# Three edits to a convolution and routed-experts kernel: smaller matmul tiles for the last 15 blocks, fp32r transposes of the expert pages, and five scatters a round

## The chip, the cores and the metric

The kernel runs on one core of a Trainium2 chip. A time is the device time of one launch in microseconds (us). The core has a matrix engine (TensorE, PE in the profile, with its weight loads listed apart as PEld), a vector engine (VectorE, DVE), an activation engine (ScalarE, ACT), a general one (GpSimd, POOL) and SyncE (SP), which here only issues transfers. Sixteen DMA engines move data between HBM and the on-chip memory SBUF. Matmuls write to PSUM, from which ACT and DVE copy.

## The reference

Two layers, one after the other, all in float32.

1. A long convolution for a batch of 4 sequences of 10048 positions and 128 channels: a filter is made by a small network from position embeddings (`relu(pos_emb @ w1) @ w2`, times a decaying window), `u = x * v` is convolved with it along the sequence by a Fourier transform of length 2 * 10048, and the result is multiplied by `x`.
2. Routed experts over the resulting 40192 tokens of 128 channels: a token chooses one of 4 groups by the largest of 4 logits, then one of that group's 4 experts, and its output is `g_w * e_w * (relu(x @ w1[g, e]) @ w2[g, e])`, with 1024 hidden units; the weights are the two softmax values of the choice.

## The kernel before

**The transform.** A sequence is cut into 79 blocks of 128 positions (10112, padded). The Fourier transform of length 157 * 128 is done in two factors: first over the 79 blocks (matrices `fa`, `fm`, `fr`), then over the 128 positions in a block (`c_b`). A channel's 79 blocks are split as 64 + 15, so that a channel's 64 main blocks fill half of the 128 rows of TensorE; the 15 that are left over are packed for three channels into one set of rows.

**Stages.** The filter's spectrum is made first. Then for each batch element b = 0..3 the kernel runs a *channel stage* and a *frequency stage*, and at the end one more channel stage for the last inverse:

- Channel stage (the loop over `OUTS`, lines 262 to 283). `OUTS` has 22 units of channels: 20 of six and two of four. They are worked in 11 pairs. For a pair the kernel transposes the back-transformed data of batch b-1 (`turned`, L704 and L707), runs the first factor of batch b for the pair's two units (`dft_unit`, L416 and L423), and the inverse first factor of batch b-1 (`inverse_rest`, L719; `inverse_blocks`, L740). The product `x * v` and its folding run a few units ahead on DVE (`run_ahead`, L487, L496, L497).
- Frequency stage (`middle` and `back`, 40 steps of two of the 79 frequencies): second factor (L506), multiplication by the filter's spectrum on DVE (L672, L675), sums on POOL (L673, L676), inverse second factor (L685), copy back on ACT (L692). The routing of the tokens of the batch element before runs inside it (`chosen`, `ranked`).

`dft_unit` writes a unit of six channels to two PSUM banks, three channels each. Its main part issues 12 matmuls (L416), each of 64 rows by 64 columns, 158 columns of the moving matrix `fm`. Its rest (L423) issues four matmuls of 64 by 64, in which one set of rows holds the 15 left-over blocks of three channels and the moving matrix `fr` has 3 * 158 = 474 columns, zero but for the blocks of the channel in question. In the profile a matmul of float32 operands shows as two records, each of all its columns. Then four copies take the result from PSUM: two main parts on ACT, two rests on DVE (L438).

**Scatters.** When the tokens of a batch element are ranked, their rows (130 numbers: the token, its place, its weight) are scattered by POOL into `prow`, a memory of pages sorted by expert. There are 79 scatters to a batch element, 128 rows each (L383), and `scatter(n)` sends up to n that are due. They are written into the program between the other work: in the channel stage one ahead of each unit and `1 + (j >= 6)` after each unit (line 274), so four to a pair in the first three pairs and six in each later one; in the frequency stage one in three of every four steps. POOL takes its work in the order of the program: a scatter that is late holds up the sums L673 and L676 behind it. A scatter also waits for the last copy written ahead of it (`pace`). By counting the turns in the code, 54 of a batch element's 79 scatters are written into the channel stage (0, 2, 4 and then 6 in each of 8 pairs) and 25 into the first 33 steps of the frequency stage. They are the rows of the batch element two before, so this concerns b = 2 and 3; the scatters of the last two elements fall into the last channel stage and the experts.

**Experts.** A page is 512, 384 or 256 rows of one expert. `load` brings it to SBUF (`xg`), `turn` transposes it 128 rows at a time (L1306, one matmul with the page as weights and the identity as the moving matrix), `rows` splits the transposed tokens into a high part in fp32r and a low part, and `first` and `second` (L1351 to L1353, L1371 to L1373) form every product as three fp32r matmuls of the parts. `turn_back` transposes the result (L1385). Every PE instruction of this phase keeps the order written down.

**Matrices.** `fm` and `fr` are loaded by POOL's queue at the top of the program (L556, L557), among the loads that the filter's network waits for.

Of the kernel before, what the change touches and what calls it, by code (L numbers as in the profile page):

```python
# [77 lines left out]
def make_consts():  # L78
# [14 lines left out]

    fr = np.zeros((2, KM, 2, GD, 2 * NB))
    for i in range(GD):
        fr[:, 16 * i : 16 * i + NB - KM, :, i] = fa[KM:].reshape(-1, 2, 2 * NB)
# [61 lines left out]
class Kernel:  # L158
# [62 lines left out]
    def conv(self, ctx, right):  # L221
# [7 lines left out]
        self.fm = cp.tile([128, 2, 2 * NB], F32, name="fm")  # L229
        self.fr = cp.tile([128, 2, GD, 2 * NB], F32, name="fr")  # L230

# [18 lines left out]
        for b in range(self.nbat + 1):  # L250
# [11 lines left out]
            for j, (d0, n) in enumerate(OUTS):  # L262
                if b > 0 and j % 2 == 0:
                    tts = self.turned(d0, min(2 * GI, D - d0))
                for i in range(j, j + 2) if not last and j % 2 == 0 else ():
                    self.run_ahead(b, i, made, folded)
                    self.scatter(1)
                    self.dft_unit(*folded[i])
                if b > 0:
                    if j % 2 == 0:  # L270
                        pos = self.inverse_rest(min(2 * GI, D - d0), tts)
                    self.inverse_blocks(b - 1, xy, d0, n, tts, pos[j % 2], j % 2)
                if not last:
                    self.scatter(1 + (j >= 6))
                if last:
                    next(weights, None)
                    if j == 8:
                        self.scatter(sum(1 for s in self.scatters if s[0] < self.nbat - 2))
                        self.all[0].load(self.rows)
                for _ in range(3 if last else 1):  # L280
                    next(routing, None)
                if last:
                    self.scatter(1 + j % 2)
# [123 lines left out]

    def dft_unit(self, b, eo, d0, n):

# [3 lines left out]
        for i in range(m):  # L413
            for h, hs in enumerate(HALVES):
                for ps, rs in zip(pss, HALVES):
                    ins = nc.tensor.matmul(  # L416
                        ps[hs, i], eo[rs, i, hs], self.fm[rs, h], start=i == 0, stop=False
                    )
                    if b and d0 == i == h == 0 and ps is pss[0]:
                        self.tc.keep_in_program_order(ins)  # L420
        for h, hs in enumerate(HALVES):
            for ps, rs in zip(pss, HALVES):
                nc.tensor.matmul(  # L423
                    ps[hs, :m].rearrange("p d k -> p (d k)"),
                    eo[rs, m, hs],
                    self.fr[rs, h, :m].rearrange("p d k -> p (d k)"),
                    start=False,
                    stop=True,
                )
        for r, ps in enumerate(pss):  # L430
            ds_ = slice(d0 + r * m, d0 + r * m + m)
# [102 lines left out]
    def network(self, ctx, eo):  # L534
# [11 lines left out]
        for j, m in groups(64, 4):  # L546
# [7 lines left out]
            if j == 16:  # L554
                nc.sync.dma_start(self.fa.rearrange("p h k -> p (h k)"), d["c_fa"])
                nc.gpsimd.dma_start(self.fm.rearrange("p h k -> p (h k)"), d["c_fm"])  # L556
                nc.gpsimd.dma_start(self.fr.rearrange("p h c k -> p (h c k)"), d["c_fr"])  # L557
        w1 = self.parts(tp, w1, "w1", lo=nc.vector)
# [522 lines left out]
    def moe(self, ctx, right, routing):  # L1081
# [4 lines left out]
        ]  # L1086
        self.sp = pools[0]
        self.weights = self.moe_weights(
            right.enter_context(tc.tile_pool(name="second", bufs=1, side="right", reuse_waits="tile")), 1
# [160 lines left out]
class Page:  # L1250
# [37 lines left out]
    def load(self, pool=None):  # L1288
        k, nc, pg = self.k, self.k.nc, self.k.pages
        self.xg = (pool or k.sp).tile([128, self.th, RW], F32, tag="xg", name="xg", bufs=1 if pool else XG)  # L1290
        at = (pool or k.sp).tile([1, 1], I32, tag="at", name="at", bufs=1 if pool else 4)
        k.tc.keep_in_program_order(nc.vector.tensor_copy(at, pg.entry(*self.at)[:, 1:2]))
        row = nc.sync.value_load(at, min_val=0, max_val=pg.none)
        src = k.d["prow"][self.skip :][ds(row, self.rows_)]
        ins = nc.sync.dma_start(self.xg, src.rearrange("(p h) c -> p h c", h=self.th))
        k.tc.keep_in_program_order(ins)
# [4 lines left out]
    def turn(self):  # L1301

        k, nc = self.k, self.k.nc
        self.px = k.psx.tile([128, self.rows_], F32, tag="px", name="px")
        for h in range(self.th):
            k.fix(nc.tensor.transpose(self.px[:, h * 128 : h * 128 + 128], self.xg[:, h, 0:128], k.ident))  # L1306

    def rows(self):
# [8 lines left out]
        self.weight = k.sp.tile([128, self.th], F32, tag="wt", name="wt", bufs=4)  # L1317
        k.fix(nc.vector.tensor_copy(self.to, self.xg[:, :, 128]))
        k.fix(nc.vector.tensor_copy(self.weight, self.xg[:, :, 129]))

# [116 lines left out]
def layout(x, v, pos_emb, w1, w2, moe_w_group, moe_w_expert, moe_w1, moe_w2):  # L1437
# [44 lines left out]

    def unit(a, n):

        u = np.zeros((2, KM, n + 1, 2, 128), np.float32)
        for r in range(2):
            u[r, :, :n] = a[:KM, r * n : r * n + n]
            u[r, : 16 * n, n] = a[KM:, r * n : r * n + n].transpose(1, 0, 2, 3).reshape(16 * n, 2, 128)
        return u

    m = {
        "xv_in": np.concatenate([unit(xv[:, d0 : d0 + n], n // 2).ravel() for xv in xvs for d0, n in OUTS]),
        "x_out": c(
# [38 lines left out]
```

## Time and profile before

| | us |
|---|---|
| median of 3 runs | 1886.09 (1885.25 to 1890.03) |
| the profiled execution: its own time | 1890.19 |
| its span in the profile | 1888.4 |
| PE busy | 1796.0 (95%) |
| DVE busy | 1362.8 (72%) |
| ACT busy | 1237.2 (66%) |
| POOL busy | 977.0 (52%) |

A busy PE is not a PE at its peak: a matmul's record lasts from its start until its last result, and the next begins before that. So the cost of a matmul is read from the distance between starts, not from its mean duration. The granted clock of TensorE in the rows is a share of 2.4 GHz.

### The profile page before, as it was taken

Reading aid. Unit: us, or ns where it says so; the run is one execution under the profiler, and the core shown is the slowest. Engines: PE = TensorE matmul, PEld = TensorE weight load, DVE = VectorE, ACT = ScalarE, POOL = GpSimd, SP = SyncE. Lnnn points to the kernel's source line nnn. Section 1 sums busy time; section 2 is a strip of 40 time slices with the busy share of each in tenths; the row PEclk is TensorE's granted clock in tenths of the full one; section 3 lists DMA queues with packets and bytes.
Section 4 is the critical chain, followed back from the end, with each engine's and each line's share of the span. In section 5 each row is a group of like instructions: output and inputs, shape, how many; then the busy total and the mean of one; then the engine's idle time right before and its main releaser. Section 6 shows DMA issues by size and latency. Waiting matters only on the chain.

```text
span 1888.4 us, 43889 instructions
## 1 busy us (share of the span) xinstructions
PE 1796.0 (95%) x14662; PEld 1489.7 (79%) x14662; DVE 1362.8 (72%) x3068; ACT 1237.2 (66%) x2708; POOL 977.0 (52%) x1105
## 2 busy tenths in 40 slices
PE   7988999999989898988899999999999999999998
PEld 6866888777867686776688888888888888889998
DVE  5385777688758874873779877777777777777886
ACT  5474367436734574456677777777777777777886
POOL 3101820574899478967255556677666333333354
PEclk9999999999989998999899999999999999999999
DMA  4477975986889688865563333444443223222342
GB/s 135 141 281 261 306 242 167 315 265 222 264 294 307 212 275 284 304 210 188 179 210 113 112 111 122 156 135 135 123 132 117 90 89 91 89 87 84 97 130 90
DMA packets 201596, 338.18 MB, mean 179 GB/s; under 512 B 26904, under 2 KB 88445, under 8 KB 201360
## 3 DMA queue, kind: packets, MB, share of 16 engines
q1 hardware_dynamic: 170448, 274.87, 45.5%
q0 software_dynamic: 21408, 44.88, 6.7%
q10 hardware_dynamic: 9504, 15.54, 2.9%
q8 instruction: 118, 1.93, 0.4%
q14 instruction: 118, 0.97, 0.2%
HBM read 260.22 MB, written 75.53 MB: 178 GB/s over the span
## 4 chain that ended last, share of the span: by engine, by line
PE 53%; DVE 2%; ACT 1%; issue 1%; DMA 0%; SPq 0%; POOL 0%; ACTq 0%; DVEq 0%; POOLq 0%
PE py L1373 8%; PE py L1371 8%; PE ph L1351 8%; PE ph L1353 8%; PE py L1372 8%; PE ph L1352 8%; PE ptm L1385 2%; PE px L1306 2%; PE po L740 1%; PE po L719 1%; PE ptr L821 1%; DMA wf<-m_w 0%; PE pt L707 0%; PE plt L829 0%; ACT tt L709 0%
## 5 line engine op out<-in xcount | busy, mean ns | idle before, releaser
L1360 DVE SCALAR_TENSOR_TENSOR hl<-ph,hh 128x512 fp32r<-128x512 f32 (+1 forms) x656 | 441.6, 674 | 157.3 <-ACT hh L1359 152.2
L1397 POOL DMA_INDIRECT out<-os,to x320 | 318.4, 995 | 415.9 <-ACT os L1392 343.0
L1359 ACT ACTIVATE hh<-ph 128x512 fp32r<-128x512 f32 (+1 forms) x656 | 388.1, 592 | 170.4 <-PE ph L1353 140.1
L383 POOL DMA_INDIRECT prow<-stg,adr x316 | 331.5, 1049 | 133.3 <-issue 68.1
L1351 PE MATMUL ph<-xh,wh 128*128 128x512 f32 (+2 forms) x720 | 280.4, 389 | 6.0 <-ACT wh L1333 6.0
L1353 PE MATMUL ph<-xh,wl 128*128 128x512 f32 (+2 forms) x720 | 265.5, 369 | 1.6 <-DVE ep L1268 1.3
L1371 PE MATMUL py<-hh,wh 128*128 128x512 f32 (+2 forms) x720 | 264.5, 367 | 0.0
L1373 PE MATMUL py<-hh,wl 128*128 128x512 f32 (+2 forms) x720 | 264.4, 367 | 0.0
L1352 PE MATMUL ph<-xl,wh 128*128 128x512 f32 (+2 forms) x720 | 264.3, 367 | 0.0
L1372 PE MATMUL py<-hl,wh 128*128 128x512 f32 (+2 forms) x720 | 263.2, 366 | 0.0
L673 POOL TENSOR_TENSOR y<-t 128x256 f32<-128x256 f32 (+1 forms) x160 | 120.5, 753 | 210.1 <-DVE t L672 205.7
L692 ACT COPY z<-pbp 128x512 f32<-128x512 f32 x128 | 74.9, 585 | 190.0 <-PE pbp L685 190.0
L506 PE MATMUL psb<-z,bt 128*128 128x256 f32 x640 | 168.2, 391 | 28.9 <-issue 15.4
L685 PE MATMUL pbp<-y,bp 128*128 128x256 f32 x632 | 164.2, 383 | 3.4 <-POOL y L676 3.1
L672 DVE TENSOR_TENSOR t<-psb,ht 128x512 f32<-128x512 f32 (+1 forms) x160 | 108.8, 680 | 75.4 <-POOL y L676 21.8
L506 PEld LDWEIGHTS psb<-z,bt 128*128 128x128 f32 x640 | 119.3, 198 | 52.3 <-issue 27.5
L1353 PEld LDWEIGHTS ph<-xh,wl 128*128 128x128 f32 x720 | 136.3, 189 | 24.0 <-DVE ep L1268 1.8
L1351 PEld LDWEIGHTS ph<-xh,wh 128*128 128x128 f32 x720 | 136.6, 190 | 22.3 <-ACT wh L1333 6.7
L1372 PEld LDWEIGHTS py<-hl,wh 128*128 128x128 f32 x720 | 135.9, 189 | 21.8
L1373 PEld LDWEIGHTS py<-hh,wl 128*128 128x128 f32 x720 | 135.8, 189 | 21.8
L1371 PEld LDWEIGHTS py<-hh,wh 128*128 128x128 f32 x720 | 135.9, 189 | 21.3
L1352 PEld LDWEIGHTS ph<-xl,wh 128*128 128x128 f32 x720 | 137.1, 190 | 15.9
(230 smaller groups left out, 3480.9 us busy)
## 6 DMA issues: line engine op xcount, KB each, us to landing
ws<-m_w SPq DMA_DIRECT2D x180, 256.0 KB
xv<-xv_in SPq DMA_DIRECT2D x80, 512.0 KB
ht<-hspec SPq DMA_DIRECT2D x156, 256.0 KB
bt<-c_b SPq DMA_DIRECT2D x95, 256.0 KB
bp<-c_bp SPq DMA_DIRECT2D x76, 256.0 KB
xyd<-xy SPq DMA_DIRECT2D x76, 256.0 KB
stg<-xyd SPq DMA_DIRECT2D x76, 256.0 KB
xg<-prow SPq DMA_DIRECT2D x66, 260.0 KB
```

Source lines behind the costliest of these rows:

```text
L383: ins = self.nc.gpsimd.indirect_dma_start(self.d["prow"], bass.IndirectOffsetOnAxis(ap=u.adr[:, t : t + 1], axis=0), u.rows[:, t - u.t0], ...
L506: nc.tensor.matmul(ps[:, i].rearrange("p s d -> p d s"), bt[:, i], self.frequency(k0 + i, 1)[:, :, 0], start=True, stop=True,)
L685: nc.tensor.matmul(by_part[:, i], bp[:, i], y[:, i], start=True, stop=True,)
L1351: k.fix(nc.tensor.matmul(ph[:, j], wh, self.xh, start=True, stop=False))
L1352: k.fix(nc.tensor.matmul(ph[:, j], wh, self.xl, start=False, stop=False))
L1353: k.fix(nc.tensor.matmul(ph[:, j], wl, self.xh, start=False, stop=True))
L1359: k.fix(nc.scalar.activation(hh, ph, AF.Relu))
L1360: k.fix(nc.vector.scalar_tensor_tensor(hl, ph, 0.0, hh.bitcast(F32), ALU.max, ALU.subtract))
L1371: k.fix(nc.tensor.matmul(self.py, wh, hh, start=(c == 0), stop=False))
L1372: k.fix(nc.tensor.matmul(self.py, wh, hl, start=False, stop=False))
L1373: k.fix(nc.tensor.matmul(self.py, wl, hh, start=False, stop=(c == NC - 1)))
L1397: ins = k.nc.gpsimd.indirect_dma_start(k.d["out"], bass.IndirectOffsetOnAxis(ap=self.to[:, h : h + 1], axis=0), o, None, bounds_check=k.nt ...
```

## The change

- The rest of the first factor is issued once for a pair of units. `dft_unit` is split into `dft_main`, `dft_rest` and `dft_leave`. The four PSUM banks of the two units each get a row group of 32: eight matmuls of 32 rows by 64 columns with 2 * 158 columns for the first two channels of each bank, then, where units have three channels to a bank, eight of 16 rows by 64 columns with 158 columns for the third. `fr` and the layout of the input follow (`both` in place of `unit`). The copies of both units come after the rest.
- The transposes of a page's tokens (`turn`) take fp32r operands: `xg` is an fp32r tile, an fp32r copy of the identity is made once, and `px` is fp32r in PSUM. Those who read them afterwards read the same bits as float32.
- `fm` and `fr` are loaded by SP's queue, behind the loads of the filter's network.
- In the channel stage `scatter(1 + j % 2)` takes the place of `scatter(1 + (j >= 6))`: five to every pair.

```diff
-                for i in range(j, j + 2) if not last and j % 2 == 0 else ():
-                    self.run_ahead(b, i, made, folded)
-                    self.scatter(1)
-                    self.dft_unit(*folded[i])
+                if not last and j % 2 == 0:
+                    units = []
+                    for i in range(j, j + 2):
+                        self.run_ahead(b, i, made, folded)
+                        self.scatter(1)
+                        units.append(self.dft_main(*folded[i]))
+                    self.dft_rest(b, units)
...
-                    self.scatter(1 + (j >= 6))
+                    self.scatter(1 + j % 2)
...
+    def dft_rest(self, b, units):
+
+        nc = self.nc
+        (one, _, m, low), (two, _, _, high) = units
+        banks = [(ps, slice(32 * g, 32 * g + 32)) for g, ps in enumerate(low + high)]
+        k = min(m, 2)
         for h, hs in enumerate(HALVES):
-            for ps, rs in zip(pss, HALVES):
+            for ps, rs in banks:
                 nc.tensor.matmul(
-                    ps[hs, :m].rearrange("p d k -> p (d k)"),
-                    eo[rs, m, hs],
-                    self.fr[rs, h, :m].rearrange("p d k -> p (d k)"),
+                    ps[hs, :k].rearrange("p d k -> p (d k)"),
+                    one[rs, m, hs],
+                    self.fr[rs, h, :k].rearrange("p d k -> p (d k)"),
                     start=False,
-                    stop=True,
+                    stop=m == k,
                 )
+        for h, hs in enumerate(HALVES) if m > k else ():
+            for ps, rs in banks:
+                rs = slice(rs.start, rs.start + 16)
+                nc.tensor.matmul(ps[hs, k], two[rs, m, hs], self.fr[rs, h, 0], start=False, stop=True)
+        for _, d0, m, pss in units:
+            self.dft_leave(b, d0, m, pss)
...
             if j == 16:
                 nc.sync.dma_start(self.fa.rearrange("p h k -> p (h k)"), d["c_fa"])
-                nc.gpsimd.dma_start(self.fm.rearrange("p h k -> p (h k)"), d["c_fm"])
-                nc.gpsimd.dma_start(self.fr.rearrange("p h c k -> p (h c k)"), d["c_fr"])
+            if j == 60:
+                nc.sync.dma_start(self.fm.rearrange("p h k -> p (h k)"), d["c_fm"])
+                nc.sync.dma_start(self.fr.rearrange("p h c k -> p (h c k)"), d["c_fr"])
...
+        self.identr = self.sp.tile([128, 128], F32R, tag="identr", name="identr", bufs=1)
+        nc.scalar.copy(self.identr, self.ident)
...
-        self.px = k.psx.tile([128, self.rows_], F32, tag="px", name="px")
+        px = k.psx.tile([128, self.rows_], F32R, tag="px", name="px")
         for h in range(self.th):
-            k.fix(nc.tensor.transpose(self.px[:, h * 128 : h * 128 + 128], self.xg[:, h, 0:128], k.ident))
+            k.fix(nc.tensor.transpose(px[:, h * 128 : h * 128 + 128], self.xg[:, h, 0:128], k.identr))
+        self.px = px.bitcast(F32)
```

## Rows read from the trace of the kernel before

**Rows 1.** Busy by stretch: length, PE, PEld, DVE, ACT, POOL (records), clock, DMA, GB/s.

```profile
133.20:178.80 45.60, 41.01 (x684) 30.85 (x680) 28.15 (x68) 26.43 (x95) 0.00 (x0) 0.96 0.81 285
...
250.10:332.90 82.80, 82.79 (x1617) 67.31 (x1617) 58.60 (x144) 61.93 (x129) 0.49 (x1) 1.00 0.63 188
332.90:429.90 97.00, 92.42 (x579) 71.47 (x577) 76.40 (x160) 40.87 (x94) 63.00 (x83) 1.00 0.89 292
...
516.90:626.20 109.30, 95.76 (x581) 72.75 (x577) 79.62 (x160) 41.43 (x95) 99.45 (x126) 0.95 0.91 297
...
937.00:1750.00 813.00, 812.82 (x3897) 676.63 (x3896) 613.20 (x1295) 614.16 (x1248) 418.07 (x439) 1.00 0.38 119
```

**Rows 2.** Timeline, one pair of b = 2: start, length, engine, line, operation, records.

```profile
471.11 1.86 PE L740 MATMUL po<-fi,tt 128*64 128x79 f32 x48
...
477.94 0.98 PE L719 MATMUL po<-fi,tt 64*64 64x158 f32 x24
...
478.86 1.86 PE L740 MATMUL po<-fi,tt 128*64 128x79 f32 x48
...
480.65 0.55 PE L704 MATMUL pt<-ident,zr 128*128 128x128 f32 x3
...
482.30 0.97 ACT L709 COPY tt<-pt 128x384 f32<-128x384 f32 x2
...
482.44 1.04 PE L416 MATMUL psa<-fm,eo 64*64 64x158 f32 x24
...
483.29 0.98 PE L423 MATMUL psa<-fr,eo 64*64 64x474 f32 x8
...
484.09 0.99 PE L416 MATMUL psa<-fm,eo 64*64 64x158 f32 x24
...
484.89 0.98 PE L423 MATMUL psa<-fr,eo 64*64 64x474 f32 x8
```

**Rows 3.** Timeline of POOL in the channel stage of b = 2.

```profile
451.02 1.42 POOL L383 DMA_INDIRECT prow<-stg,adr  x1 [21.39 <-ACT oo L750]
...
469.45 0.98 POOL L383 DMA_INDIRECT prow<-stg,adr  x1 [0.30 <-ACT z L438]
...
516.38 0.98 POOL L383 DMA_INDIRECT prow<-stg,adr  x1 [0.30 <-DVE zr L438]
```

**Rows 4.** Timeline, start of the frequency stage of b = 2; in brackets the idle time before.

```profile
530.45 0.74 POOL L673 TENSOR_TENSOR y<-t 128x256 f32<-128x256 f32 x1
...
532.01 2.04 PE L506 MATMUL psb<-z,bt 128*128 128x256 f32 x4 [7.71 <-issue]
```

**Rows 5.** Timeline of PE, frequency stages of b = 1 and of b = 2.

```profile
350.50 1.02 PE L685 MATMUL pbp<-y,bp 128*128 128x256 f32 x4
...
543.74 1.02 PE L685 MATMUL pbp<-y,bp 128*128 128x256 f32 x4
```

**Rows 6.** Chain that ended last: four transposes of one page.

```profile
1044.59 0.44 PE px L1306 x4
```

**Rows 7.** Weight loads by line: total busy, mean ns of one, idle before.

```profile
L1351 PEld LDWEIGHTS ph<-xh,wh 128*128 128x128 f32 x720 | 136.6, 190 | 22.3 <-ACT wh L1333 6.7
...
L1306 PEld LDWEIGHTS px<-ident,xg 128*128 128x128 f32 x320 | 40.0, 140 | 8.9
...
L1062 PEld LDWEIGHTS pe<-ident,lst 128*1 128x1 f32 x20 | 0.7, 82 | 3.2 <-DVE yt L754 2.8 <-issue 0.4
```

**Rows 8.** Timeline of PE in a page of 256 rows.

```profile
1820.13 0.28 PE L1351 MATMUL ph<-xh,wh 128*128 128x256 f32 x1
1820.25 0.28 PE L1352 MATMUL ph<-xl,wh 128*128 128x256 f32 x1
```

**Rows 9.** Timeline of ACT at the start of the program.

```profile
9.05 0.46 ACT L524 CAST p<-pt 128x320 fp32r<-128x320 f32 x1 [3.24 <-DMA pt<-pos_t]
```

**Rows 10.** DMA issues: the size of `fr`.

```profile
fr<-c_fr POOLq DMA_DIRECT2D x1, 474.0 KB
```

**Rows 11.** Busy time by stretch at the start of the program.

```profile
6.00:8.00 2.00, 0.90 (x2) 0.50 (x2) 0.43 (x2) 0.00 (x0) 0.00 (x0) 1.00 0.98 327
```

More of the change, by code (lines that the diff above doesn't have):

```diff
@@ L91, in make_consts @@
     ).reshape(NB, -1)
-    fr = np.zeros((2, KM, 2, GD, 2 * NB))
-    for i in range(GD):
+    fr = np.zeros((4, 32, 2, 2, 2 * NB))
+    for i in range(2):
         fr[:, 16 * i : 16 * i + NB - KM, :, i] = fa[KM:].reshape(-1, 2, 2 * NB)
@@ L229, in conv @@
         self.fm = cp.tile([128, 2, 2 * NB], F32, name="fm")
-        self.fr = cp.tile([128, 2, GD, 2 * NB], F32, name="fr")
+        self.fr = cp.tile([128, 2, 2, 2 * NB], F32, name="fr")
         self.z = zp.tile([128, D, KM, 2], F32, name="z")
@@ L406, in clear, with dft_main @@
         return ins
-    def dft_unit(self, b, eo, d0, n):
+    def dft_main(self, b, eo, d0, n):
         nc, m = self.nc, n // 2
@@ L420, in dft_unit, with dft_leave @@
                         self.tc.keep_in_program_order(ins)
+        return eo, d0, m, pss
+    def dft_rest(self, b, units):
[3 more added lines that the diff above has]
+        k = min(m, 2)
         for h, hs in enumerate(HALVES):
-            for ps, rs in zip(pss, HALVES):
+            for ps, rs in banks:
                 nc.tensor.matmul(
-                    ps[hs, :m].rearrange("p d k -> p (d k)"),
-                    eo[rs, m, hs],
-                    self.fr[rs, h, :m].rearrange("p d k -> p (d k)"),
+                    ps[hs, :k].rearrange("p d k -> p (d k)"),
+                    one[rs, m, hs],
+                    self.fr[rs, h, :k].rearrange("p d k -> p (d k)"),
                     start=False,
-                    stop=True,
+                    stop=m == k,
                 )
+        for h, hs in enumerate(HALVES) if m > k else ():
[4 more added lines that the diff above has]
+            self.dft_leave(b, d0, m, pss)
+    def dft_leave(self, b, d0, m, pss):
+        nc = self.nc
         for r, ps in enumerate(pss):
@@ L1289, in load @@
         k, nc, pg = self.k, self.k.nc, self.k.pages
-        self.xg = (pool or k.sp).tile([128, self.th, RW], F32, tag="xg", name="xg", bufs=1 if pool else XG)
+        self.xg = (pool or k.sp).tile([128, self.th, RW], F32R, tag="xg", name="xg", bufs=1 if pool else XG)
         at = (pool or k.sp).tile([1, 1], I32, tag="at", name="at", bufs=1 if pool else 4)
@@ L1294, in load @@
         src = k.d["prow"][self.skip :][ds(row, self.rows_)]
-        ins = nc.sync.dma_start(self.xg, src.rearrange("(p h) c -> p h c", h=self.th))
+        ins = nc.sync.dma_start(self.xg.bitcast(F32), src.rearrange("(p h) c -> p h c", h=self.th))
         k.tc.keep_in_program_order(ins)
@@ L1317, in rows @@
         self.weight = k.sp.tile([128, self.th], F32, tag="wt", name="wt", bufs=4)
-        k.fix(nc.vector.tensor_copy(self.to, self.xg[:, :, 128]))
-        k.fix(nc.vector.tensor_copy(self.weight, self.xg[:, :, 129]))
+        k.fix(nc.vector.tensor_copy(self.to, self.xg[:, :, 128].bitcast(F32)))
+        k.fix(nc.vector.tensor_copy(self.weight, self.xg[:, :, 129].bitcast(F32)))
     def matrix(self, i, half, e):
@@ L1481, in layout, with both @@
     xvs = np.stack([xb[:, :, q], vb[:, :, q]]).transpose(1, 2, 4, 0, 3)
[L1483 to L1489, printed above, removed]
+    def both(xv, d0, n):
+        k, parts = n // 2, []
+        a = xv[:, d0 : d0 + 2 * n]
+        for second in range(2):
+            u = np.zeros((128, k + 1, 2, 128), np.float32)
+            for r in range(2):
+                o = second * n + r * k
+                u[64 * r : 64 * r + KM, :k] = a[:KM, o : o + k]
+            for g in range(4):
+                for i in range(2 * second, min(2 * second + 2, k)):
+                    o = 32 * g + 16 * (i % 2)
+                    u[o : o + NR - KM, k] = a[KM:, g * k + i]
+            parts.append(u.ravel())
+        return np.concatenate(parts)
     m = {
-        "xv_in": np.concatenate([unit(xv[:, d0 : d0 + n], n // 2).ravel() for xv in xvs for d0, n in OUTS]),
+        "xv_in": np.concatenate([both(xv, d0, n) for xv in xvs for d0, n in OUTS[::2]]),
         "x_out": c(
```

## The prediction

> **What bounds the kernel now.** I read the busy time by stretch first, cut where the timeline of PE changes from one stage to the next [rows 1]. The reader is to see five kinds of stretch. In the experts (937 to 1750) PE is busy for 812.8 of 813 us while DVE, ACT and POOL have a fourth or more to spare: whatever PE is spared there comes off the time. In a channel stage that also has an inverse (250.1 to 332.9) PE is busy throughout as well. In the first channel stage (133.2 to 178.8), which has no inverse, PE has 4.6 us to spare and the DMA engines are at 0.81. The frequency stage takes 97.0 us for b = 1 and 109.3 for b = 2; the second has 99.5 us of POOL in it, at a mean granted clock of 0.95. Last, the start of the program, where ACT waits 3.24 us for a load of the network [rows 9].
>
> Then the timeline of one pair [rows 2]. The inverse L740 begins at 471.11 and again at 478.86: a pair takes 7.75 us. PE's starts follow one another without a hole: L719 at 477.94, L740 at 478.86, transposes at 480.65, main part 482.44, rest 483.29, second main part 484.09, second rest 484.89, and by the period the next L719 at 485.69. So a rest costs 0.80 us, of 474 columns in two rounds: 0.80/948 = 0.844 ns a column, with the four matmuls of a round side by side.
>
> **Part 1, the rest of the transform.** Now: two rests, 1.60 us a pair. After: eight tiles side by side would give two rounds of 316 and two of 158 columns, 948 * 0.844 = 0.80 us; saving 0.80.
>
> Against that stand changes of the tile's shape. A 64x64 rest follows a 64x64 main part with no loss, but L719 (24 records, six rounds of 158 columns, 0.80 us by the same rate) lasts 0.92 until the 128x64 of L740 begin, and the 15 transposes last 1.79 where four take 0.44 us [rows 6], that is 1.65 for 15: 0.12 and 0.14 us at a change. The new rest has a change ahead of it and one behind it, 0.26 us a pair. The Trainium skill, TensorEngine Tiling (Array Packing), section Tiling Modes, says why: changing the tiling mode, not just the tile, drains the engine. The rows agree with it; without that rule one would count the whole 0.80.
>
> Whether eight tiles run side by side no row shows; four do. If PE takes records no faster than in the main part (24 in 0.80 us, 33 ns each), 32 records take 1.06 us and the saving is 1.60 - 1.06 - 0.26 = 0.28 us. If only four run at a time, the rest stays at 1.60 and the pair loses 0.26. With all eight it is 0.54. I take 0.43, between the two in which the smaller tiles help, since in [rows 2] nothing binds the main part but its columns. From this goes 0.1: the second main part writes the PSUM buffers of the first two transposes, whose copies end at 482.30 + 0.97 = 483.27; it now wants them at 483.29 rather than 484.09, and a copy is not seen at once. 0.33 us a pair remain.
>
> The copies out of PSUM (L438) of a pair's first unit now start 1.6 us later. Their cover is PE's work on L719 and L740, 2.7 us, before the first inverse result is there for ACT; if that cover were gone, L740's copies and so the next PSUM buffers would be late.
>
> Pairs: 11 for each b, ten with three channels to a bank. For b = 1: 10 * 0.33 + 0.1 = 3.4 us. For b = 0 I take 0.5 (0 to 5): PE isn't the bound there.
>
> **Part 2, the scatters.** In [rows 3] the scatters start at 451.02, and from 469.45 to 516.38 there are 34, so 33 steps in 46.93 us: 1.42 us each, the small copies (L375) among them. Six to a pair are 8.5 us of POOL in 7.75 us of PE. POOL falls behind, and [rows 4] show what comes of it: the channel stage ends at 516.9 [rows 1], but POOL's first sum L673 runs at 530.45, 13.5 us later, and PE meanwhile sits idle, 7.71 us at once. A landmark that both frequency stages have is the step whose L685 stands in [rows 5]: 17.6 us after the start for b = 1 (350.50 - 332.9), 26.8 for b = 2. So the delay is 9.2 us; from there the stages run at the same pace until the last steps.
>
> After: by the turns in the code 48 scatters (0, 3, then nine times 5) stand in the channel stage, 30 in the frequency stage, and one is left for the next. Five to a pair are 7.1 us of POOL, in a pair of 7.4. POOL is through at 451.0 + 48 * 1.42 = 519.2, the stage ends at 516.9 - 3.4 = 513.5: 5.7 us of lag in place of 13.5. I take 6.5 of the 9.2 us as gained (4 to 9). The five scatters that are added to the frequency stage fall into its last steps, where none stood; they are 6.5 us of POOL at the nearest step in [rows 3] of 1.28 us without a copy, beside DVE's ranking. I take 1.5 (0 to 6.5). For b = 2: 3.4 from part 1, 6.5 - 1.5 here, 8.4 us; b = 3 has some longer pairs that DVE holds, I take 7.6. Together 16 us.
>
> **Part 3, the transposes of the pages.** 320 of them (the count of [rows 7]), 0.44/4 = 0.11 us each [rows 6], in a stretch where PE is the bound. They are 128 columns at the 0.83 ns a column that float32 has here. No fp32r matmul under 256 columns is in the trace; one of 256 starts 0.12 us after the one before [rows 8], which is 0.47 ns a column. In proportion 128 columns are 0.06 us; with the 0.107 us that 256 columns take at one column a period of 2.4 GHz and a fixed 0.013 beside it, 0.067. I take 0.068. The weights must keep up: a load for a transpose lasts 140 ns, one for a product 190, one of a single column 82 [rows 7], so the transpose's load adds 58 ns for its columns and fits, the product's adds 108 and would not. I expect the transposes to keep the shorter load: 0.110 - 0.068 = 0.042 us, times 320 = 13.4 us (0 to 16 on this side). A loss can't be excluded: twice the present columns' rate would be 0.21 us and cost 33 us. The fp32r copy of the identity is one copy of ACT, under 1 us, beside the waits at the start of the experts.
>
> **Part 4, the matrices.** `fr` is 474 KB [rows 10] and `fm` a third of it by its shape, 632 KB at 327 GB/s [rows 11]: 1.9 us of the DMA engines, which are at 0.98 just while ACT waits 3.24 us [rows 9]. The later loads stand where SP has nothing else in its queue but the filter's matrices, 90 us ahead of their use. I take 1.7 us (0 to 3).
>
> **Sum.** 1.7 + 0.5 + 3.4 + 16 + 13.4 = 35.0 us. The profiled execution took 1890.19 us (span 1888.4): 1855.2. The median of the runs is 4.1 us below it, so the forecast for the median is **1851 us**.
>
> **Rivals.**
>
> *The transposes gain nothing* (20%). For: loads of 128 columns add 108 ns in every fp32r product of [rows 7], and at that the load, not the 128 columns, sets the pace, as now. Against: the transposes' own load adds 58. Time: 1851 + 13 = 1864. The Trainium skill, TensorE: Matmul & The Clock Gate, section on LDWEIGHTS, gives the load as its columns over 1.2 GHz, 107 ns for 128, whatever the type; by that rule alone this rival would hold. The trace agrees for products and differs for transposes.
>
> *Only four of the small tiles run at once* (10%). For: no row shows more than four. Against: in [rows 2] tiles of different rows and columns already run together. A pair then loses 0.26 + 0.1 us; b = 1 loses 3.9 in place of 3.4 gained, the channel stages of b = 2 and 3 lose as much, but as the scatters then have more room their lag is gone: 9.2 - 1.5 - 3.9 = 4 each. 1.7 + 0 - 3.9 + 8 + 13.4 = 19: 1867.
>
> *The scatters come back in the frequency stage* (7%). For: POOL is at 99 of 109 us there. Against: DVE's ranking already holds the last steps. All 6.5 us would be paid, twice 5 more than I count: 1861.
>
> *fp32r is slow on short operands* (8%), the one on the other side. In `turn`, 320 times: for it speaks only that every fp32r matmul in the trace has 256 columns or more; against it that the 256 columns of [rows 8] cost 0.12 us, close to one column a period, with no sign of a step below. If 128 cost 0.21 us each, the experts lose 33 us in place of 13 gained, and 1886 - 21.6 + 33 = 1897. It decides from 0.18 us a transpose on, where the other gains (21.6 us / 320 = 0.07) are used up.
>
> The forecast itself has 55%.
>
> **How the numbers follow.** What a measurement can tell from no change is about 0.3%, 5.7 us. Forecast, first three rivals: all faster by more, 92%; the last 8% is mostly slower; for mishaps that no row shows I move some to no change: faster 0.88, within 0.3% 0.05, slower 0.07. The range: at the low end all parts at their best ends, eight tiles at 0.54, the transposes at 16, the start at 3 and the lag gone, 48 us, 1838; at the high end it holds the first three rivals and some of two together, 1872. Left out are the last rival and the sums of several.
>
> **What would show it.** In the chain or timeline of the experts four transposes L1306 in about 0.27 us and each page of 512 rows shorter by 0.17 us. In a pair of b = 1 the period at 7.4 us, with one rest of about 1.2 us behind both main parts, switches included. In b = 2 the first L673 some 6 us after the first L506, and the frequency stage near 104 us. At the start the second copy of `pt` near 7.2 us. Wrong it would be if four transposes take 0.44 us or more, if the pair stays at 7.75, or if POOL's first sum is still 10 us late.

## The result, and the profile of the kernel after

After the change: 1863.06 us, median of 4 runs (1860.53 to 1864.3), beside 1885.67 of before on the same chip (4 runs, 1884.48 to 1890.03): the ratio of the runs is put at 0.9874, 95% interval [0.9855, 0.9893]. It is 22.6 us faster, where 35 were forecast. The profiled execution took 1863.25 us (span 1861.4); that of before was 4.5 us above its median, so the two traces differ by 27.0 us in their spans.

In two of the three jobs below (e1 to e4, e9 to e12) every kernel, that of before too, took some 10% longer for a reason that no trace shows (before 2075 and 2077 us; of the 210 us that the trace of e9 is longer than that of after, 72 lie in the channel stages of b = 2 and 3, whose pairs mostly take 8 to 15 us there, and 128 in the experts). So these times stand beside before of the same job only, and of those traces I read only what agrees with the others: what lies ahead of the scatters of b = 2, the frequency stages from POOL's first sum on, and the pages without a stall.

Lines are those of the kernel after: L419 main part, L434 and L444 the new rest, L741 and L762 the inverse, L527 and L707 the frequency stage, L695 and L698 POOL's sums, L386 the scatter, L1330 the transposes of a page. Where the 27.0 us lie, from the starts of the stages in both traces (first transposes of each channel stage at 250.1, 429.9, 626.2, 823.1 before and 241.3, 417.1, 612.1, 803.4 after):

| stretch | forecast | measured |
|---|---|---|
| start to the first product of the filter's second factor (86.1, now 78.9) | 1.7 | 7.2 |
| from there to the first transposes of b = 1 | 0.5 | 1.6 |
| b = 1 (179.8, now 175.9) | 3.4 | 3.9 |
| b = 2 (196.3, now 195.0) | 8.4 | 1.3 |
| b = 3 (196.8, now 191.2) | 7.6 | 5.6 |
| last channel stage, to the first page (89.0, now 86.7) | 0 | 2.3 |
| experts, to the end (976.3, now 971.3) | 13.4 | 5.0 |

The stretches of after that answer to [rows 1], in the same columns:

```profile
241.30:320.35 79.05, 79.05 (x1777) 66.77 (x1777) 59.41 (x144) 61.03 (x128) 0.44 (x1) 1.00 0.65 198
320.35:417.15 96.80, 92.45 (x580) 71.51 (x578) 76.41 (x160) 40.92 (x94) 63.12 (x83) 1.00 0.88 290
417.15:502.60 85.45, 81.92 (x1776) 68.72 (x1776) 66.36 (x163) 61.20 (x128) 48.24 (x53) 0.96 0.79 242
502.60:612.15 109.55, 95.83 (x582) 72.54 (x578) 84.87 (x167) 41.13 (x95) 98.39 (x123) 0.97 0.90 298
...
911.00:1720.00 809.00, 807.45 (x3886) 669.42 (x3885) 614.72 (x1296) 613.13 (x1245) 415.12 (x440) 1.00 0.38 120
```

The reader is to see two things. The channel stage of b = 1 shrank from 82.80 to 79.05 us with PE busy throughout. The frequency stage of b = 2 kept its length (109.3, now 109.55), though its first sum comes much earlier. One count goes with that: the scatters that POOL still runs inside this stage, before and after (length, POOL with its records, clock, DMA, GB/s):

```profile
516.95:626.24 109.29, 35.14 (x36) 0.95 0.91 297
```

```profile
502.61:612.15 109.54, 35.73 (x35) 0.97 0.90 298
```

One of the 36 began before the stage, so it is 35 both times. Before, 10 of them ran ahead of the first sum and 25 between the sums, after 5 and 30. A pair of b = 2, answering to [rows 2]:

```profile
482.43 0.55 PE L726 MATMUL pt<-ident,zr 128*128 128x128 f32 x3
...
484.22 1.91 PE L419 MATMUL psa<-fm,eo 64*64 64x158 f32 x48
486.06 0.79 PE L434 MATMUL psa<-fr,eo 32*64 32x316 f32 x16
486.64 0.48 PE L444 MATMUL psa<-fr,eo 16*64 16x158 f32 x16
487.05 1.04 PE L741 MATMUL po<-fi,tt 64*64 64x158 f32 x24
488.02 1.86 PE L762 MATMUL po<-fi,tt 128*64 128x79 f32 x48
489.81 0.55 PE L726 MATMUL pt<-ident,zr 128*128 128x128 f32 x3
```

From 482.43 to 489.81 the pair takes 7.38 us. L434 lasts 0.58 us to the next start for 632 columns, 0.92 ns each: eight tiles do run side by side (with four at a time these would be 1264 columns in the same 0.58 us, 0.46 ns each, about half of the 0.844 that float32 has in [rows 2]).

POOL and PE in the frequency stage of b = 2, its start (to set beside [rows 4]) and its end:

```profile
509.15 0.75 POOL L695 TENSOR_TENSOR y<-t 128x256 f32<-128x256 f32 x1
```

```profile
604.29 1.13 PE L707 MATMUL pbp<-y,bp 128*128 128x256 f32 x4 [1.08 <-POOL y L698]
607.68 1.13 PE L707 MATMUL pbp<-y,bp 128*128 128x256 f32 x4 [2.26 <-POOL y L698]
610.46 1.22 PE L707 MATMUL pbp<-y,bp 128*128 128x256 f32 x2 [1.65 <-POOL y L698]
```

The first sum runs 6.5 us after the stage's start (502.6) in place of 13.5, as forecast. But at the end PE now waits 5.0 us for POOL in three pieces, where the scatters have been put between the last sums. In before the last steps have one such wait:

```profile
623.79 1.97 PE L685 MATMUL pbp<-y,bp 128*128 128x256 f32 x6 [1.03 <-POOL y L676]
```

Behind the three waits the granted clock is 0.50 over into the channel stage of b = 3, whose first pair takes 8.92 us in place of 7.30:

```profile
612.15:615.40 3.25, 3.25 (x15) 3.06 (x15) 3.25 (x13) 1.65 (x3) 1.64 (x3) 0.50 0.84 238
```

The transposes of a page: loads and products of one page of 512 rows.

```profile
1021.87 0.14 PEld L1330 LDWEIGHTS px<-identr,xg 128*128 128x128 f32 x1
1021.96 0.14 PEld L1330 LDWEIGHTS px<-identr,xg 128*128 128x128 f32 x1
1022.04 0.14 PEld L1330 LDWEIGHTS px<-identr,xg 128*128 128x128 f32 x1
1022.13 0.19 PEld L1376 LDWEIGHTS ph<-xh,wh 128*128 128x128 f32 x1
```

```profile
1021.87 0.46 PE L1330 MATMUL px<-identr,xg 128*128 128x128 f32 x4
1022.17 0.46 PE L1376 MATMUL ph<-xh,wh 128*128 128x512 f32 x1
1022.47 0.39 PE L1377 MATMUL ph<-xl,wh 128*128 128x512 f32 x1
```

Four transposes and the product behind them take 0.60 us (1021.87 to 1022.47); in the trace of before the same five take 0.68:

```profile
1044.42 0.60 PE L1306 MATMUL px<-ident,xg 128*128 128x128 f32 x4
1044.78 0.48 PE L1351 MATMUL ph<-xh,wh 128*128 128x512 f32 x1
1045.10 0.40 PE L1352 MATMUL ph<-xl,wh 128*128 128x512 f32 x1
```

The load behind each transpose's load starts 0.087 us after it, and the product cannot start before its own load, the last of these.

### The profile page after: what moved, and what is told of

Its sections match the earlier page's. It is cut to its first block, busy times and chain, and to the rows that moved or that the text cites. A ratio compares the mean times of both kernels' runs of the same rounds, so it can differ in the third digit from the quotient of the medians.

```text
span 1861.4 us, 45165 instructions
## 1 busy us (share of the span) xinstructions
PE 1781.0 (96%) x15302; PEld 1481.9 (80%) x15302; DVE 1373.1 (74%) x3068; ACT 1234.1 (66%) x2709; POOL 967.8 (52%) x1103
## 4 chain that ended last, share of the span: by engine, by line
PE 78%; DVE 7%; DMA 3%; issue 3%; POOL 2%; ACT 2%; SPq 0%; DVEq 0%; ACTq 0%; POOLq 0%
PE ph L1376 8%; PE py L1398 8%; PE ph L1378 8%; PE py L1396 8%; PE ph L1377 8%; PE py L1397 8%; PE psb L527 5%; PE pbp L707 5%; PE po L762 3%; PE psa L419 3%; PE pt L729 2%; PE po L741 2%; PE ptm L1410 2%; PE ptr L843 2%; PE psa L434 1%
## 5 line engine op out<-in xcount | busy, mean ns | idle before, releaser
L386 POOL DMA_INDIRECT prow<-stg,adr x316 | 322.0, 1019 | 139.1 <-issue 65.9
L1376 PE MATMUL ph<-xh,wh 128*128 128x512 f32 (+2 forms) x720 | 279.8, 389 | 5.8 <-ACT wh L1358 5.8
L695 POOL TENSOR_TENSOR y<-t 128x256 f32<-128x256 f32 (+1 forms) x160 | 121.7, 760 | 204.5 <-DVE t L694 201.9
L527 PE MATMUL psb<-z,bt 128*128 128x256 f32 x640 | 165.5, 386 | 16.3 <-DVE hs L669 5.6
L707 PE MATMUL pbp<-y,bp 128*128 128x256 f32 x632 | 165.8, 384 | 11.8 <-POOL y L698 9.4
L1376 PEld LDWEIGHTS ph<-xh,wh 128*128 128x128 f32 x720 | 136.8, 190 | 21.9 <-ACT wh L1358 6.2
L527 PEld LDWEIGHTS psb<-z,bt 128*128 128x128 f32 x640 | 117.1, 195 | 39.6 <-issue 16.5
```

The costliest lines, as they stand in the source:

```text
L386: ins = self.nc.gpsimd.indirect_dma_start(self.d["prow"], bass.IndirectOffsetOnAxis(ap=u.adr[:, t : t + 1], axis=0), u.rows[:, t - u.t0], ...
L527: nc.tensor.matmul(ps[:, i].rearrange("p s d -> p d s"), bt[:, i], self.frequency(k0 + i, 1)[:, :, 0], start=True, stop=True,)
L707: nc.tensor.matmul(by_part[:, i], bp[:, i], y[:, i], start=True, stop=True,)
L1376: k.fix(nc.tensor.matmul(ph[:, j], wh, self.xh, start=True, stop=False))
```

## The experiments

**One part of the change alone (e1 to e4), on the kernel before.**

e1, only the transposes:

```diff
-        self.xg = ...tile([128, self.th, RW], F32, ...)
+        self.xg = ...tile([128, self.th, RW], F32R, ...)
...
-            k.fix(nc.tensor.transpose(self.px[:, ...], self.xg[:, h, 0:128], k.ident))
+            k.fix(nc.tensor.transpose(px[:, ...], self.xg[:, h, 0:128], k.identr))
```

> The kernel before with the fp32r transposes alone. Theory (the weight load sets their pace: in the trace of after the loads of four transposes follow one another 0.087 us apart, and four transposes with the product behind them take 0.60 us in place of 0.68): 320 * 0.022 = 7 us less, so about 1879 beside 1886 (5 to 8 less). The forecast's 0.042 us each: 13.4 less, 1872. Rival, no gain at all: 1886.

Measured 2076.91 beside 2075.44 (ratio 1.0016 [0.999, 1.0041]): in that job no difference can be told. In its trace 36 undisturbed pages of 512 rows start 11.785 us apart on average; in before 62 such pages 11.845. That is 0.060 us for four transposes, 0.015 each, times 320 = 4.8 us; the experts of after were 5.0 us shorter. Below the theory's 7, far below the forecast's 13.4. The theory counted four shorter steps of 0.022 us to a page; the rows of the loads have three (the first load of a page runs under the product ahead of it, and from the product's own load to the next it is 0.11 as before), 0.066 us in all.

e2, only the matrices:

```diff
-                nc.gpsimd.dma_start(self.fm..., d["c_fm"])
...
+            if j == 60:
+                nc.sync.dma_start(self.fm..., d["c_fm"])
...
```

> The kernel before with only the later loads of the two matrices. Theory (the 7.2 us by which the network's end came earlier after the change are all theirs): 7 us less, 1879 (5 to 9 less). The forecast's 1.7 us: 1884. Rival, the start gained from something else: 1886.

2069.81 beside 2075.44 (0.9977 [0.9948, 1.0006]). The first product of the second factor starts at 79.3 us; in e1 and e4, which load both matrices at the top, at 85.5 and 87.2, in before at 86.1. So the later loads alone give some 7 us at the start, as the theory had it; that the time fell too is not clear of the interval.

e3, only the rest:

```diff
-                    self.dft_unit(*folded[i])
...
+                        units.append(self.dft_main(*folded[i]))
+                    self.dft_rest(b, units)
```

> The kernel before with only the new rest of the first factor. Theory A (POOL never rests from the first scatter of b = 2 and 3 to the end of their frequency stages, so what PE saves in these channel stages is not seen): only b = 0 and 1 gain, some 5 us less, 1881 (3 to 7 less), and the period from the first transposes of b = 2 to those of b = 3 stays at 196 us. Theory B (PE's saving counts for each b, as forecast): 10.7 us less, 1875, and that period 193.

2099.4 beside 2075.44 (1.0132 [1.0097, 1.0167]). Both theories had it faster; the loss lies in the channel stages of b = 2 and 3, and no other job shows it, so nothing is built on it. What can be read: b = 1 takes 176.5 us against 179.4 to 180.7 in e1, e2 and e4, with pairs of 7.38 against 7.75. And the first product of the second factor is at 81.8, 4 to 5 us earlier than in e1 and e4, though both matrices are still loaded at the top: the new `fr` is 316 KB in place of 474.

e4, only the scatters: `1 + j % 2` for `1 + (j >= 6)`.

> The kernel before with only five scatters to a pair. Theory A (POOL's queue is the bound over the whole of b = 2 and 3, and moving scatters inside it changes nothing but the one that is left over): 0 to 4 us less, 1884. Theory B (the delay of the first sums, 6.5 us for each of two batch elements, is gained and 1.5 given back): 10 us less, 1876. Theory C (the tail gives more back than the start gains): slower than 1886.

2057.28 beside 2075.44 (0.9914 [0.9882, 0.9945]), a gain that again rests on the long pairs of that job. From POOL's first sum to the end the frequency stages of b = 2 and 3 take 101.6 and 100.3 us, with 30 scatters in them; in e1, with 25, 96.4 and 95.8.

**One part undone, or taken further (e5 to e8), on the kernel after.** In this job before took 1883.72, and after at its ratio would take 1860.

e5, the old rest, as in the diff of the change read backwards.

> The kernel after with the old rest of the first factor (four tiles of 64 by 64 for each unit), all else as after. Times are for a chip on which before takes 1886 and after 1863; on another chip the same differences. Theory A (in the trace of after POOL never rests from the first scatter of b = 2, at 439.5, to the end of the frequency stage, so PE's saving in the channel stages of b = 2 and 3 is hidden): only b = 0 and 1 lose, 4 to 6 us, 1868. Theory B (the saving counts for each b): 11 us, 1874.

1871.81 (0.9939 [0.9922, 0.9955]), 0.0065 above after's ratio, with both intervals 12 us (7 to 17). By the times theory B holds. The traced execution, the fastest of its four, is 3.5 us longer than that of after: b = 1 4.3 us longer, b = 2 0.1, b = 3 1.9, the start 2.8 shorter. In b = 2 the rest's gain was lost not to POOL, as theory A said, but in one pair: the channel stage is as long in e5 as in after (85.47 and 85.46 us). The second pair of after (start, length, idle before):

```profile
424.83 0.60 PE L729 MATMUL pt<-ident,z 128*128 128x128 f32 x4
428.96 1.97 PE L729 MATMUL pt<-ident,z 128*128 128x128 f32 x8 [3.53 <-DVE zr L459]
430.86 3.44 PE L419 MATMUL psa<-fm,eo 64*64 64x158 f32 x48
434.23 0.98 PE L434 MATMUL psa<-fr,eo 32*64 32x316 f32 x16
```

and, by stretch, TensorE's clock in it (columns as in [rows 1]):

```profile
430.90:434.20 3.30, 3.30 (x49) 2.72 (x48) 2.20 (x4) 0.59 (x1) 0.00 (x0) 0.50 0.77 247
```

The same place in e5:

```profile
429.48 0.66 PE L708 MATMUL pt<-ident,z 128*128 128x128 f32 x4 [2.05 <-DVE zr L438]
430.35 0.66 PE L708 MATMUL pt<-ident,z 128*128 128x128 f32 x4 [0.21 <-DVE zr L438]
```

The transposes need PSUM buffers that DVE's copies `zr` of the pair before set free. In the new form all these copies come after both units; here DVE has the end of the ranking (L933 to L944) in its queue ahead of them, and PE waits 3.53 us instead of 2.26:

```profile
427.30 0.20 DVE L944 CAST adr<-pos 128x79 int32<-128x79 f32 x1
...
428.67 0.40 DVE L459 COPY zr<-psa 128x90 f32<-128x90 f32 x2
```

Behind that wait the granted clock is 0.50, the lower level, and the two main parts take 3.37 us in place of 1.84. The pair lasts 13.7 us; in the five traces with the old rest 10.4 to 12.1, in seven others with the new one (all but e12) 12.6 to 13.9.

Not all of this is the new form's. In before, whose waits in this pair are those of e5 (2.05 and 0.21 us), the clock fell behind them as well:

```profile
440.70 0.66 PE L707 MATMUL pt<-ident,z 128*128 128x128 f32 x4 [2.05 <-DVE zr L438]
```

```profile
442.62:444.25 1.63, 1.63 (x25) 1.55 (x28) 1.56 (x4) 0.59 (x1) 0.00 (x0) 0.50 0.62 211
```

Its pair takes 12.0 us. In six traces of the new form the clock is low for as long as in before, and the pair takes 12.65 to 12.68. So the late copies cost some 0.7 us there; the rest of the 3.3 us between after (13.7) and e5 (10.45) goes with how long the clock was low, twice as long in after as in before and not at all in e5.

e6, the old count of scatters.

> The kernel after with the old count of scatters, 1 + (j >= 6), all else as after. Theory A (POOL's queue is the bound of b = 2 and 3, in whichever order it has its work): within 4 us of after, 1865. Theory B (the delay of the first sums comes back and counts, 5 us for each of two): 1873. Theory C (the late scatters in the frequency stage cost more than the early delay): under 1863.

1868.95 (0.9926 [0.9909, 0.9942]), 10 us (5 to 15) above after; by the times theory B, by the trace, again the fastest of its four and 2.4 us longer than after's, theory A. Its frequency stages are 109.7 and 108.5 us, those of after 109.5 and 107.4: the first sum comes late,

```profile
516.69 0.74 POOL L695 TENSOR_TENSOR y<-t 128x256 f32<-128x256 f32 x1
```

14.4 us after the start at 502.3, but from there on the stage takes 95.3 us, in after 103.0. So within this stage the edit is worth nothing; in e6 too 35 or 36 scatters run inside the stage. What the untraced runs of e6 lost beyond that stays open.

e7, the first scatters earlier:

```diff
-                        self.scatter(1)
+                        self.scatter(4 if j == 2 else 1)
...
-            self.scatters += [(b, ..., self.tick + LAGS, u) ...]
+            self.scatters += [(b, ..., self.tick + 1, u) ...]
```

> The kernel after with the first scatters of a batch element sent earlier: due one turn after their addresses are made in place of three, and four in the unit j = 2 of the second pair, so that POOL starts some 11 us earlier and eight scatters leave the frequency stage. Theory A (POOL's queue from its first scatter on sets the end of the frequency stage): 8 to 11 us less for each of b = 2 and 3, 1845. Theory B (PE and DVE set the end of the frequency stage, POOL is only busy beside them): 1863.

1849.77 (0.981 [0.979, 0.9831]), 12 us (7 to 17) less than after and the fastest of all. POOL's first scatter, first sum, and the frequency stage of b = 2:

```profile
432.34 1.22 POOL L386 DMA_INDIRECT prow<-stg,adr  x1 [11.60 <-issue]
...
512.42 0.74 POOL L695 TENSOR_TENSOR y<-t 128x256 f32<-128x256 f32 x1
```

```profile
505.90:607.20 101.30, 93.89 (x580) 72.53 (x578) 78.08 (x160) 40.91 (x94) 91.23 (x116) 0.98 0.92 310
```

POOL starts 11.3 us after the first transposes (after: 22.4), and 23 scatters are left between the sums in place of 30. The stages take 101.3 and 101.7 us, from the first sum on 94.7 and 95.2. So theory A holds for 30 scatters, where POOL has the last word, and not far below (in the last steps PE waits 1.0 to 1.2 us for POOL in e7, as it does in b = 1 without a scatter): by the traces b = 2 gained 8.9 us as expected, b = 3 only 3.5 of the 8 to 11.

e8, with the small copies on ACT as well:

```diff
-            self.beyond(self.nc.gpsimd.tensor_copy(u.rows[:, :n, 128:130], ...))
+            self.beyond(self.nc.scalar.copy(u.rows[:, :n, 128:130], ...))
```

> As the kernel with the earlier scatters, and the small copies into the staging tiles moved from POOL to ACT: 20 copies to a batch element, 0.36 us of POOL each with the wait behind them (0.18 + 0.17 in the trace of after), 7 us. Theory A: b = 2 and 3 come near the period of b = 1, which has no scatters (176 us, against 195 and 191), but not below some 182: 1863 - 13 - 9 = 1841 (1834 to 1848). Theory B: 1863.

1854.98 (0.9844 [0.9828, 0.9861]), slower than e7 by 6 us (1 to 11):

```profile
418.40:504.40 86.00, 82.43 (x1777) 68.62 (x1777) 66.98 (x164) 63.03 (x144) 52.38 (x52) 0.98 0.79 255
504.40:606.60 102.20, 94.63 (x580) 72.49 (x578) 79.37 (x160) 41.47 (x99) 87.60 (x108) 0.98 0.91 306
```

POOL has 3.6 us less work in the stage than in e7 (87.60, 91.23) and the stage is no shorter: POOL no longer sets its end. In the channel stage, where ACT's copies free PSUM, pairs grew from 7.38 to 7.47 and 7.60; that the small copies delay those others is likely, but not shown.

**The last four (e9 to e12).**

e9, the kernel after once more.

> The kernel after once more, as the mark for the three others of this job: 22 to 26 us less than before, 1861 beside 1884. Theory: in the frequency stages of b = 2 and 3 the first of POOL's sums comes 6.5 us after the start and the rest of the stage takes 101 to 103 us, as in its first trace.

2078.26 beside 2076.54 (0.9995 [0.9967, 1.0023]): in that job the change is worth nothing. The 22 to 26 us expected were missed. Why is open: there is no trace of before from that job to set beside this one. From the first sum on its stages take 101.5 and 99.9 us with 30 scatters (101 to 103 were expected), but that sum comes 4.6 and 4.5 us after the start, not 6.5, with three scatters ahead of it in place of five.

e10, after with float32 transposes; the diff of e1 read backwards.

> The kernel after with the transposes of the pages in float32 again. Theory (the load of the weights, 0.087 us, sets the pace of the fp32r transposes, so that four of them with the product behind take 0.60 us in place of 0.68): 6 us more than after (5 to 8), 1867. The forecast's 0.042 us each: 13.4 more, 1874. Rival, no difference: 1861.

2082.75 (1.0024 [0.9993, 1.0056]), 4.5 above e9, inside both intervals. Its pages start 11.842 us apart, those of e9 11.778: 0.064 us for four transposes, 5 us for 320, as in e1.

e11, after with the matrices loaded early again; the diff of e2 read backwards.

> The kernel after with the two matrices on POOL's queue at the top again. Theory (six traces with the later loads have the first product of the second factor at 78 to 79 us, four without at 82 to 87): 6 to 8 us more than after, 1868, and that product back at 85 us. The forecast's size: 1.7 us more, 1863.

2079.24 (0.9996 [0.9964, 1.0029]). The product that was to fall back to 85 us starts at 80.4, 1.4 us later than in e9 (79.0): the forecast's size, not the theory's. ACT's second copy `p`, beside [rows 9]:

```profile
7.58 0.46 ACT L545 CAST p<-pt 128x320 fp32r<-128x320 f32 x1 [2.17 <-DMA pt<-pos_t]
```

In the kernel after it is:

```profile
6.05 0.46 ACT L545 CAST p<-pt 128x320 fp32r<-128x320 f32 x1 [0.55 <-DMA pt<-pos_t]
```

So part 1 (the smaller `fr`, e3) and part 4 (the later loads, e2) each take away most of the same loss: either alone 4 to 7 us, both 7.

The traces also show what the loss is. The network has two layers, and PE's products for them (`psh`, then `psg`) alternate. The last `psh` starts at 36.7 us in before and at 35.7 in after, 1.0 apart, but the last `psg` at 50.2 and 43.1, 7.1 apart. The order is why: behind the last `psh` stand 78 records of `psg` in before and 48 in after (length, PE, PEld, DVE, ACT, clock, DMA, GB/s of what touches `psg`):

```profile
36.76:50.90 14.14, 10.69 (x78) 9.00 (x78) 2.92 (x7) 7.04 (x21) 1.00 0.04 13
```

```profile
35.80:43.80 8.00, 6.67 (x48) 5.52 (x48) 1.71 (x5) 4.53 (x13) 1.00 0.01 2
```

This order of `psh` and `psg` is the same to the last record in the three traces with the old loads and the old `fr` (before, e1, e4: 78), in the two with the old loads and the new `fr` (e3, e11: 54), and in the two with the later loads and the old `fr` (e2, e5: 48), on whatever chip: it belongs to the program and not to the execution. So the changed loads gave the program another order, and 6 of the 7 us are its shorter tail.

e12, e7 with no scatter after the units of the last pair:

```diff
-                    self.scatter(1 + j % 2)
+                    self.scatter((1 + j % 2) * (j < 20) + (j == 11))
```

(One more stands at j = 11.)

> The kernel with the earlier scatters, and none after the units of the last pair: 54 scatters in the channel stage, ending before its end, and 25 in the frequency stage. Theory A' (25 scatters beside the sums are free, from the first sum to the end of the stage 94 to 96 us with 0 to 25 of them and 101 to 103 with 30; what is left is the delay of the first sum, 6.5 us with five scatters ahead of it and 2.6 with none): first sum at 3 to 4 us, stages of 98 to 99 us, 3 us less for each of b = 2 and 3 than with the earlier scatters alone: 16 less than after, 1845. Theory B' (each scatter costs its 1.2 us wherever it stands): as the earlier scatters alone, 10 to 13 less than after, 1850.

2094.92 beside 2076.54 (1.0079 [1.0051, 1.0108]); the loss is again in the channel stages, where its second pair, the one with the eight early scatters, takes 19 to 20 us (12.7 and 13.7 in e7, which has them too), so nothing is built on it. The first sum comes at 2.9 us, near the 3 to 4 expected, but the rest of the stage takes 98.7 and 98.3 us, not 94 to 96: what is gained ahead of the first sum comes back behind it. Theory A' holds for the first sum and falls for the total.

**What the stages say together.** From the first sum to the end, over the traces: with no scatter (b = 1) 94 to 96 us; with 22 to 25 (all but e12) 94.5 to 96.4; with 30 99.9 to 103.1. Between the sums some 25 scatters cost next to nothing, and the next five 4 to 8 us; with these five PE waits 3.0 to 5.0 us for POOL in the last 30 us of the stage, with 25 or fewer 1.0 to 1.2.

But e12 does not fit this, since its 25 scatters go with 98.7 and 98.3 us. A count that leaves no trace out is that of all scatters begun inside the stage, ahead of the first sum or behind it, beside the whole stage's length: none, 97 to 99 us; 25 to 28 (e7, e8, e12) 101.2 to 102.2; 29 or 30 (e1, e2, e3) 101.4 to 105.2; 33 (e4, e9, e10, e11) 104.4 to 107.5; 35 or 36 (before, after, e5, e6) 106.7 to 109.7. So the first 25 cost some 0.15 us each, each one beyond them some 0.8, and on which side of the first sum they stand hardly matters. It is a count made afterwards, and what sets the 101 to 102 us of e7 and e12 is not shown.

## Why the prediction was right in its time and wrong in its parts

The time lies in the range, 12 us above the forecast, but that is partly luck. By the table above b = 2, b = 3 and the experts gave 17.5 us less than forecast, and the other stretches 9.4 more, 5.5 of them at the start. Without these the time would have been some 1872, the end of the range. The 2.3 us of the last channel stage no run accounts for.

**Part 1 was right in size.** 0.33 us a pair were forecast, 0.37 measured. Eight tiles side by side, and the changes of shape are there: the two main parts take 1.84 us where two old ones took 1.65, and L444 0.41 for 316 columns that would be 0.27 by the rate. The rival with only four tiles is out. But "Their cover is PE's work on L719 and L740" failed in the second pair of b = 2 (e5): the copies L438, now late, stand behind DVE's ranking. This cost the pair 0.7 us where the clock was low as long as in before, and 1.7 in the trace of after (13.7 against 12.0), where it was low for longer.

**Part 2 failed in one step:** "The five scatters that are added to the frequency stage fall into its last steps ... I take 1.5 (0 to 6.5)". The gain ahead of it was right (13.5 to 6.5 us, 7.0; I took 6.5). The price in b = 2 was all of it, 95.8 to 103.0 us, 7.2; in b = 3 it was 5.1 of 6.9 (to 100.9), and the fallen clock took another 1.6 from the first pair of b = 3. That is my third rival, "All 6.5 us would be paid", with its 7%. That its time of 1861 is close to what came out is chance: it has the other parts as forecast. The step behind it is that I counted the delay of the first sum as the cost. POOL has 35 scatters left to run in the stage before and after; five of them were moved from ahead of the first sum to behind it, and the stage's length goes with their number. I had argued that DVE's ranking holds the last steps anyway. The three waits of PE for POOL above show that POOL holds them once scatters stand there, and e7, which takes seven of the 35 out of the stage, has its stages at 101 us.

**Part 3 was between the forecast and the first rival.** I took 0.068 us a transpose, from the columns, and expected the loads to keep up because one row lasts 140 ns. The row kept its length (141 ns), but loads start 0.087 us apart, more than the 0.068, so they set the pace; page by page 0.015 us of the 0.042 were gained (e1, e10), 5 us of 13.4. The rival of a slow fp32r, at twice the old rate, is out. In the old trace the loads of the transposes are 0.11 us apart, as the float32 columns are; how fast they can follow, it did not show. The Trainium skill, TensorE: Matmul & The Clock Gate, section on LDWEIGHTS, would have 107 ns for 128 columns and so no gain; the trace agrees for a product, behind whose load the next starts after 0.11 us (L1376), and has 0.087 for the transposes.

**Part 4 was mis-sized in a sum of two.** 1.7 us were forecast for the start and 7.2 came. Undoing the loads alone costs 1.4 (e11), because the smaller `fr` of part 1 had already cured most of it (e3: 4 to 5 us). I had counted `fr` as if it were only moved, not shrunk. The 2 to 3 us of a late second copy grow to 7 by the end of the network because the program's order changed with the loads: 78 records of the second layer are left behind the first in before, 48 in after. My sum had only the time of the DMA engines, and no row that I read shows the order.

The change was faster by more than 0.3%, as the 0.88 had it.

## What to carry to other kernels

An engine that shares a stage with others has a capacity for extra work that costs little (here some 25 scatters of 1.2 us made 97 to 99 us into 101 to 102; each further one cost some 0.8). To take away the wait at the start of a stage gains nothing if the same work then stands at its end: count all that the engine has left to do in the stage, and what the last steps hold, since little covers them. Work moved later also moves behind whatever the other engines have queued meanwhile, so a cover that holds for the usual pair has to be checked in the unusual one. Two edits that cure the same wait do not add. And an edit to a load can change the order of the whole program behind it, so compare the order of records in both traces and not only the waits.

## What was not expected of the hardware

- A row's length of a weight load does not tell how fast loads follow one another: 140 ns rows at 0.087 us for the transposes, 190 ns rows at 0.11 for the products.
- After 3.53 us in which PE waited (busy 0.04 of 3.50 us) the granted clock was 0.50 for the next 3.3 us; after 2.05 us of waiting in e5 it stayed at 1.00, but in before the same waits (2.05 and 0.21 us) were followed by 0.50. The length of one wait does not tell which comes.
